# W_tok padded to 640 x 640 in a fused linear-attention and MLP kernel, with a new order for the whole program

## The chip, the cores and the metric

The kernel runs on one core of a Trainium2 chip. The core has a matrix engine (TensorE, PE in the profile; its weight loads are listed as PEld), three engines for elementwise work (VectorE or DVE, ScalarE or ACT, GpSimd or POOL) and DMA queues that are fed by SP, ACT and POOL. In this kernel matmuls write to PSUM, which the code holds as eight banks of 128 x 512 float32, and ACT and VectorE read it from there; POOL does not. The metric is the device time of one execution in microseconds (us).

## The reference

Eight batches of 576 tokens pass through linear attention with eight heads of 64 columns and then through a block that mixes tokens and channels:

```python
kv = np.einsum('bhsd,bhse->bhde', k, v)
out = np.einsum('bhsd,bhde->bhse', q, kv)
rms = np.sqrt(np.mean(out * out, axis=-1, keepdims=True) + 1e-06)
attn = out / rms * g_norm                   # heads side by side: x, 576 x 512
a1 = alpha1 * x + beta1
tok = np.einsum('ts,bsd->btd', w_tok, a1)   # w_tok is 576 x 576
u = x + lam * tok
a2 = alpha2 * u + beta2
ch = np.maximum(a2 @ w_ch1, 0.0) @ w_ch2    # 512 -> 2048 -> 512
return u + lam * ch
```

All inputs and the output are float32. The kernel multiplies in bfloat16 from the token mixing on and in float32 forms in the attention.

## The kernel before, in words

A batch has 576 = 4 x 128 + 64 tokens. Its work comes in pieces of 128 tokens (c = 0 to 3) and a tail of 64 (c = 4); the tails of two batches, an even and the odd one after it, share one piece of 128 partitions.

For every batch `kv` forms K^T V for all heads (lines 607 and 613), and ACT and VectorE bring it from PSUM into `kvc` (624, 626). `norm` multiplies q by it (697) and `norm_ops` normalises: a square on ACT (665), a sum on VectorE (668), a root on ACT (671), a reciprocal (674) and products on VectorE (676 to 683), for some pieces one on POOL (686). `tok` multiplies by W_tok transposed (780), `tok_tail` does so for the shared tail (825). `a2_dma` scales the result (870, 874, 877), and a transposing DMA brings it into `a2m`, for the tail into `a2l`. `ch1` is the first channel matmul with its relu (890 and 885, the tail 902), `ch2` the second (919, for the last piece of the last batch 930), and `finish` adds lambda times the result and stores it (947 to 955).

Batch 0 runs in two halves of four heads (j = 0, 1) so that it can begin when a part of the inputs is there: `qt_early` copies q (556 on ACT, 559 on POOL) and transposes it on TensorE (563), ACT bringing it to `qt` (576); `kv_first` makes K^T V from 64 x 64 tiles (585; copies 595 and 597); `norm_half` (723 to 759; 759 is POOL's product that writes `rm`), `tok_half` (803) and `a2_pair`, which transposes on TensorE (845), follow. Batch 1's q too goes through `qt_early`; later batches have theirs transposed by VectorE (1090).

W_tok is loaded in three DMAs from POOL (482 twice, 485) that turn it into bfloat16. `wt_group` transposes it: for each of five groups of columns four matmuls with the identity (971) and one for the last 64 rows (974). ACT and VectorE copy the result to `wt` (981, 978, 986). `wsums` (997, 999) sums it with a matmul by `pick` and writes the sums to the upper half of `wt`'s fifth tile; two DMAs (1013) then make a sixth tile, with the halves exchanged, for odd batches. Since 576 = 4 x 128 + 64, the fifth group is 64 columns wide (its 971 fill 64 of TensorE's columns) and the last 64 rows use 64 of its rows (974, 999).

w1 is loaded in four parts (1057) and w2 in four (1063), from POOL; k and v of the batches from 1 on too, each in a large and a small part (1080, 1084). SP issues batch 0's and batch 1's q (463), batch 0's k and v (463), later q (1072), the rows of constants (517, 1115), the transposes and the stores.

What decides the order is a list by hand of a planner: `ORDER`. Every operation of the program has a number in the order in which the code makes it, and `replay` puts the operations on their engines in the order of the list. `53:5:6` is operation 53 with PSUM banks 5 and 6. `206:7+325:4` is two or three groups of matmuls whose instructions are woven with each other. `~14` is fourteen filler matmuls on a constant tile (line 447; the tile `fil` is set at 446) whose result nobody reads. Each engine, and each issuer of DMAs, runs its part of the list in that order. `GATES` makes an operation wait for another one beyond what the data need, `8: 14` operation 8 for operation 14; what stands behind 8 on its issuer then waits too.

## Time and profile before

| what | us |
|---|---|
| median of 3 runs | 349.39 (349.28 to 351.33) |
| the profiled execution's own time | 349.69 |
| its span (first to last instruction) | 347.5 |
| TensorE busy | 340.9 |
| VectorE busy | 186.4 |
| GpSimd (POOL) busy | 162.4 |
| ScalarE (ACT) busy | 153.0 |
| first ch1 matmul of batch 0 starts at | 33.13 |
| first tok matmul of batch 1 starts at | 61.51 |

A row of the timeline has the start, the duration, the engine, the line, the operation, what it writes and reads, and the count of what was merged into it; behind it, in brackets, how long the engine stood idle and what ended that. A duration of several matmuls includes the end of the last, which the profile shows beyond the start of the next, so the price of a matmul is taken from one start to the next. In the chain of waits a row has start, duration, engine, tile and line.

### The profile page before, as it was taken

Reading aid. Unit: us, or ns where it says so; the run is one execution under the profiler, and the core shown is the slowest. Engines: PE = TensorE matmul, PEld = TensorE weight load, DVE = VectorE, ACT = ScalarE, POOL = GpSimd, SP = SyncE. Lnnn points to the kernel's source line nnn. Section 1 sums busy time; section 2 is a strip of 40 time slices with the busy share of each in tenths; the row PEclk is TensorE's granted clock in tenths of the full one; section 3 lists DMA queues with packets and bytes.
Section 4 is the critical chain, followed back from the end, with each engine's and each line's share of the span. In section 5 each row is a group of like instructions: output and inputs, shape, how many; then the busy total and the mean of one; then the engine's idle time right before and its main releaser. Section 6 shows DMA issues by size and latency. Waiting matters only on the chain.

```text
span 347.5 us, 5443 instructions
## 1 busy us (share of the span) xinstructions
PE 340.9 (98%) x2188; PEld 194.2 (56%) x2188; DVE 186.4 (54%) x343; ACT 153.0 (44%) x301; POOL 162.4 (47%) x154
## 2 busy tenths in 40 slices
PE   6999999999999999999999999999999999999996
PEld 4978465456645554555646545564576444444644
DVE  3188029774882687636854776359543963210044
...
GB/s 249 349 206 304 118 224 252 163 112 209 231 93 30 172 223 195 48 95 243 194 46 130 239 202 50 60 125 272 135 36 88 60 30 17 63 90 30 0 62 91
DMA packets 108496, 48.10 MB, mean 138 GB/s; under 512 B 82029, under 2 KB 101557, under 8 KB 108472
## 3 DMA queue, kind: packets, MB, share of 16 engines
...
q8 instruction: 17, 0.28, 0.4%
...
HBM read 38.82 MB, written 9.44 MB: 139 GB/s over the span
## 4 chain that ended last, share of the span: by engine, by line
PE 91%; DVE 5%; ACT 1%; DMA 1%; issue 0%; POOL 0%; DVEq 0%
PE ps L919 31%; PE ps L890 31%; PE ps L780 9%; PE ps L902 4%; PE ps L697 2%; PE ps L607 2%; PE ps L563 2%; PE ps L825 2%; PE ps L585 1%; PE ps L803 1%; PE ps L930 1%; DVE ps L676 1%; DMA a2l<-a2b 1%; DVE small L668 1%; PE ps L447 1%; PE ps L723 1%
## 5 line engine op out<-in xcount | busy, mean ns | idle before, releaser
L919 PE MATMUL ps<-w,hh 128*128 128x512 bf16 x560 | 137.2, 382 | 0.0
L890 PE MATMUL ps<-a2m,w 128*128 128x512 bf16 x512 | 120.3, 381 | 0.0
L885 ACT ACTIVATE hh<-ps 128x512 bf16<-128x512 f32 x144 | 84.3, 596 | 69.8 <-PE ps L890 61.0
L919 PEld LDWEIGHTS ps<-w,hh 128*128 128x128 bf16 x560 | 48.3, 98 | 51.0 <-issue 1.2
L890 PEld LDWEIGHTS ps<-a2m,w 128*128 128x128 bf16 x512 | 45.8, 98 | 51.1 <-ACT a2m L855 0.5
L870 POOL TENSOR_TENSOR a1f<-xm,a_bc 128x512 f32<-128x512 f32 x24 | 30.3, 1269 | 80.7 <-DVE xm L790 80.6
L947 DVE TENSOR_TENSOR tmp<-ps,lam_bc 128x512 f32<-128x512 f32 (+2 forms) x38 | 25.0, 662 | 53.8 <-PE ps L919 50.1
L697 PE MATMUL ps<-kvc,qt 128*128 128x128 f32 x140 | 46.7, 395 | 0.1
L952 POOL TENSOR_TENSOR xm<-xm,tmp 128x512 f32<-128x512 f32 x28 | 35.5, 1272 | 22.0 <-DVE tmp L947 22.0
L877 POOL TENSOR_TENSOR a2b<-a1f,b_bc 128x512 bf16<-128x512 f32 x32 | 40.2, 1272 | 7.4 <-DVE a1f L874 7.0
L607 PE MATMUL ps<-vr,kr 128*128 128x128 f32 x112 | 35.8, 394 | 0.0
L668 DVE TENSOR_REDUCE small<-sq 128x8 f32<-128x512 f32 (+1 forms) x35 | 23.6, 679 | 22.4 <-ACT sq L665 22.3
L697 PEld LDWEIGHTS ps<-kvc,qt 128*128 128x128 f32 x140 | 26.2, 195 | 9.3 <-DVE kvc L626 1.4
L665 ACT ACTIVATE sq<-ps 128x512 f32<-128x512 f32 (+1 forms) x35 | 20.7, 596 | 20.6 <-PE ps L697 20.3
L780 PE MATMUL ps<-rm,wt 128*128 128x512 bf16 x112 | 28.9, 379 | 0.4 <-DVE rtl L681 0.4
L790 DVE TENSOR_TENSOR xm<-ps,xm 128x512 f32<-128x512 f32 x24 | 16.6, 690 | 23.0 <-PE ps L780 23.0
L1093 ACT ACTIVATE qt<-qp 128x576 fp32r<-128x576 f32 x24 | 16.0, 681 | 23.6 <-DVE qp L1090 23.6
L607 PEld LDWEIGHTS ps<-vr,kr 128*128 128x128 f32 x112 | 21.3, 196 | 6.6 <-issue 1.3
L676 DVE TENSOR_TENSOR ps<-ps,small 128x512 f32<-128x512 f32 (+1 forms) x35 | 23.5, 691 | 0.5
L626 DVE TENSOR_TENSOR kvc<-ps,kvo 64x256 fp32r<-64x256 f32 x14 | 5.9, 420 | 27.5 <-ACT kvo L624 27.4
L1090 DVE STREAM_TRANSPOSE qp<-qs 128x576 f32<-128x576 f32 x24 | 17.7, 758 | 2.2 <-ACT qt L1093 1.8
L683 DVE TENSOR_TENSOR xm<-ps,g_bc 128x512 f32<-128x512 f32 x28 | 18.1, 677 | 0.1
(123 smaller groups left out, 309.9 us busy)
## 6 DMA issues: line engine op xcount, KB each, us to landing
...
vr<-in_v_dram POOLq DMA_DIRECT2D x7, 1024.0 KB, 12.1
...
```

Source lines behind the costliest of these rows:

```text
L607: P.mm("fill", 128, [lambda e, t=t, c=c, h=h, o=128 * (h % 4): e.matmul(t.ap()[:, o:o + 128], kr4[:, h, c:c + 2, :].rearrange("p c d -> p ...
L668: P.op("DVE", dve(n), lambda e: e.tensor_reduce(out=st, in_=sq[rs, s3, 0:nst, :], axis=AX.X, op=ALU.add), r=[("sq", s3)], w=[("sm", s4)])
L676: P.op("DVE", dve(n), lambda e: e.tensor_tensor(out=grp(ps()), in0=grp(ps()), in1=st[..., None].to_broadcast([rs.stop - rs.start, nst, DH] ...
L697: P.mm("fill", 128, [lambda e, p=p: e.matmul(dst(p), qt[:, p, cs], kvc[:, i, p, :], start=(p == 0), stop=(p == 3)) for p in range(4)], r=[ ...
L780: P.mm("fill", 512, [lambda e, sc=sc: e.matmul(t.ap(), wt[:, sc if sc < 4 else tw(b), 128 * c:128 * c + 128], rsrc(b, sc, al), start=(sc = ...
L870: P.op("POOL", pool(512), lambda e: e.tensor_tensor(out=a1f[:, s], in0=x, in1=a2_bc[:], op=ALU.mult), r=ks + ["a2"], w=[("a1f", s)])
L877: P.op("POOL", pool(512), lambda e: e.tensor_tensor(out=a2b[:, c], in0=a1f[:, s], in1=b2_bc[:], op=ALU.add), r=[("a1f", s), "b2"], w=[("a2 ...
L885: P.op("ACT", act(512), lambda e: e.activation(dst, t.ap(), ACT.Relu), r=[t], w=keys, pri=-1000)
L890: P.mm("main", 512, [lambda e, dj=dj: e.matmul(t.ap(), w1[:, dj, 128 * fj:128 * fj + 128], a2m[:, b % 3, dj, :], start=(dj == 0), stop=(dj ...
L919: P.mm("main", 512, [lambda e, fj=fj, t=t, c=c: e.matmul(t.ap(), (ht[:, fj, 128 * c:128 * c + 128] if c < 4 else hl[:, fj, :]), w2[:, fj, ...
L947: P.op("DVE", dve(z - a), lambda e: e.tensor_tensor(out=tmp[:, s, a:z], in0=t.ap()[:, 0:z - a], in1=lam_bc[:, a:z], op=ALU.mult), r=[t, "l ...
L952: lambda e: e.tensor_tensor(out=x, in0=x, in1=tmp[:, s, a:z], op=ALU.add),
```

## The change

The source of W_tok in SBUF becomes 640 columns wide with five row tiles of 128. The columns from 576 on, the rows from 64 on of its last tile, and the rows from 64 on of `wt`'s fifth tile are set to zero by three new memsets on VectorE (new operations 31, 32 and 33). With that the fifth group of 971 fills all 128 columns of TensorE, and 974 and the last matmul of `wsums` use all 128 rows; line 999 is gone. Buffers `qs` and `qp` shrink to what is used.

`ORDER` and `GATES` are new as a whole. From 31 on an operation's new number is the old one plus 3. Some of it in words, by new numbers: 6 to 11 and 16 to 21 are batch 0's loads of q, k and v by SP, which were 6 7 17 9 10 19 8 16 18 11 21, batch 1's 187, and 20, and are now 7 6 9 8 11 10 17 19 18 16 21 20; 22, 23 and 24 are W_tok's loads; 48 is POOL's first copy of q; 189 to 192 are batch 1's q loads (186 to 189 before). On POOL, after W_tok's loads, came w1 in four parts, then k and v, between copies of q; now come the first two products for `rm` (79, 72), the load of v (198), a copy of q, the first part of w1 (188), a product (86), three copies of q, the second part of w1 (193), the last three products (153, 160, 167), and then k (196), the small part of v, w1's third part, the small part of k, w1's fourth and w2. The fillers were 14, 5, 4, 25, 4 and 4, and are 39, 3, 4, 2 and 1. From batch 6 on the order is the old one.

In the diff the order is cut to its beginning, and lines that only give `mm` its new argument `tile`, which nothing reads when the program is built, are left out.

```diff
 ORDER = """
-14 32 3 6 4 204 7 13 17 12 1 205 9 2 0 10 30 29 ~14 19 31 28 8 5 33 16 15 34 27 18 40:1 ~5 11 46
-45 21 42:2 26 187 127 20 35 41 186 25 49:3 189 43 37 44 47:4 39 50 36 53:5:6 48 126 124:7 51:1
-~4 125 52 132:2 188 22 128:3 133 130:4 129 23 54 131 24 134:7:1 59 55 223 60 56 61 57 62 135 185
-58 190 70:4:5 140 136 141 137 215 63:2:3 142 138 71 143 139 191 84:6 108:1 85 72 90:7 91 64 109
-~25 192 73 65 193 74 66 75 86 110 87 111 92 93 ~4 89 195 67 95 77:4 113 88:5 94 100 102:6 76 68
-103 104 105 78 96:7 97 98 99 158:1 79 101 144:2:3 107 80 69 159 81 106 112 38 116:7 160 145 82
-161 224 146 115 114 165:6 117 83 162 163 147 118 151:4:5 164 148 225:1 149 152 119:7 226 166 150
-153 229:2 168:3 120 230 167 154 169 155 216 121 227:1 156 122 ~4 217:2 228 170 157 221:6 219:7
-218 171:4 222 173:5 220 172 175:1 174 176 194 178:3 177 196 179 309:0 180 197 312:2 310:6 198
-181:7 183:4 199 182 311:5 184 316 200 314 329:1 345:3 330 335:7 346 331:4 336 315 332 321 341:1
-322 337:3 342 319 338 206:7+325:4 320 207+333:5 326 208:1+339:3 334 203 123 323 340 209+343:6
-202 324 210+327:4 231 344 313 211 317 213 347:5 232 212 328 214 318 239:3 348 255:2 240 234
-263:6+352:7 241 256 257 242 247:4+351:1+355 264 243 244 258 259 265 233 260 266 271:5+356+360
-248 245 249 246 237 238 261 250 272 350:0 251 267 262 252 235 373 268 253 359 273 254 369 269
-274 349:3 275 270 276 353 277 236 278 279:2 285:4 280 281 291:6 286 282 287 297:5 292 283 288
-293 379:2+357+361 298 289 284 294 299 295 300 290 377:4+303:6 301 296 380 304 378+354+358 302
-305 306 201 307 386 381+365 388 387 308 486:5 382 390 384 389 383 484:6 385 391 392 487 488:4
-362 393 401 394 509:2 370 399 485 468:5 363 489 366 466:3 398 469 367 374 418:6+490:1+474:4 467
-375 491 419 510 395 426:5+470:0+462:7 475 420 397 421 364 471 422 371 423 400 511 463 512 425
-499:3 504:1 396 513 402:4+476:0+492:7 424 477 403 434:2+464:6+478:0 493 404 427 405 428 505 465
-500 501 479 406 514:7 407 372 429 376 430 506 409 410:6+472:0 368 408 431 494:4 411 495 507 432
-473 496 497 508 502 412 515 503 433 435 543:0 498 436 413 544 414 437 415 535:1 438 416 480:3
-439 559 521:5 481 441 560 522 440 561 550:4+536+528:3 417 562 563 565 442:2 564 566 447:6 443
-444 529 448 452:2 449 457:6 453 445 551+537+538 458 450 446 454 451 552:2+482:6 459 553 483 554
-455 530 555 557 556 523 460 558 456 524 461 575:6+516+517 525 526 576 531 574 567 518 573 577
 ...
+13 0 3 7 1 30 4 ~39 6 207 12 9 14 27 8 2 31 11 5 33 10 29 17 28 19 32 49 18 26 16 48 25 21 23
+50:2 20 22 43:1 54:3 52:4 37 56:5:6 53 15 24 ~3 51 57 55 44 127:1 45:7 58 62 59 63 60 64 130 61
+65 ~4 128 73:4:5 46 129 66:2:3 74 38 80:6 75 67 137:1:7 81 191 68 76 192 77 138 82 69 189 70 78
+83 ~2 71 135:5 79 139 131:4 143 136 140 144 133:2 141 84 34 145 85 132 87:5 111:3 112 72 88 146
+~1 99:6 35 89 100 134 113 101 105:7 93:4 142 114 102 39 94 95 106 90 116 107 96 108 40 161:1 198
+98 92 190 147:2:3 110 162 219 104 154:4:5 163 188 148 119:7 164 149 155 86 165 156 150 227 171:6
+120 166 218 157 151 121 168:1 226 158 152 193 224:7 169 172 225 232:2 159 228:3 153 233 220:7
+170 229 91:4 222:5 173 97 160 230:2 221 103 176:3 231 109 174:1 167 177 115 181:2 118 196 175
+182 117 199 178:6 183 194 223 179 314:2 180 313:5 197 315:7 195 184:1 186:6 185 200 122:3 187
+312:0 123 316 201 208 319 320 318 124 321 317 202 326 324 322 211:1+332:3 323 212+330:6
+209:5+334:4 210+328:0 335 325 213+336:4 331 236 327 203 340:2 216 214 217 234 337 215 342:7 341
+36 47 329 242:6+344:1 343 250:5+338:0 243 333 244 345 258:4+355:7 245 246 126 247
+274:1+354:2+346:3 259 41 248 251 125 42 260 206 252 261 266:6+358 347 262 263 253 339 254 348:3
+264 275 255 267 265 359 349 205 256 353:0 268 249 276 357 269 270 257 277 271 362 272 363 237
+278 279 361 273 280 350:5 281 235 282:3 288:4 283 284 294:6 351 285 289 300:5 286 295 290 306:1
+296 291 287 301 292 352:4 297 302 204 307 368 298 293 303 308 356 304 309 299 380:6+376 310 305
+382:3+360 311 383+364 238 381+372 365 239 369 481:4 240 373 465:0 374 482 485:5 366
+384+487:4+491:1 241 385 495:2 387 386 466 377 477:6 486 388 378 488 483:5 492 496 507:0 370
+497:1 484 471:7 391 398 502:4 472 489:3 389 478 397 498 490 499 399 500 503 392 504 508 400 390
+512:2 395 473:6 393 396 505 479:7 404 394 403 501 513 514 480 413:3+469:5 474 402 515 414
+405:7+475:6 470 415 506 509 416 510 406 437:1+538:5 417 418 511 407 516 421:4+539+467:0 420 401
+408 476 409 438 410 419 429:6+540 468 439 422 411 493:3 440 430 423 546:2 441 494 442 424 541
+412 431 524:7 443 432 547 433 425 434 525 436 435 553:3+548+526 426 427 444 450:6 428 554+445:1
+451 452 555:4+455:6 446 562 447 460:1 456 563 453 564 549 461 565 556+531:0 448 568 566
+557+517:6+532 462 449 457 454 560 527 569 561 463 558 533 528 567 559 458 518 464 519 529 459
 ...
 """

-GATES = {8: 14, 9: 204, 10: 1, 11: 30, 15: 204, 20: 45, 21: 7, 22: 18, 25: 41, 26: 27, 36: 7, 37: 0,
-    38: 107, 39: 9, 122: 136, 123: 197, 185: 133, 186: 204, 187: 27, 188: 126, 189: 10, 191: 3,
-    194: 122, 196: 101, 199: 120, 201: 305, 202: 149, 231: 154, 232: 198, 233: 259, 234: 348,
-    235: 267, 236: 232, 237: 348, 238: 256, 394: 387, 396: 391, 397: 287, 400: 289, 568: 459,
-    569: 526, 571: 585, 574: 562, 678: 705, 685: 705}
+GATES = {40: 1, 41: 152, 42: 183, 125: 327, 126: 246, 191: 75, 192: 15, 205: 255, 206: 244, 235:
+    262, 237: 345, 240: 268, 397: 335, 404: 290, 570: 428, 571: 432, 572: 427, 574: 550, 681:
+    708, 688: 708, 721: 741, 725: 375, 726: 627, 894: 885, 896: 523, 897: 523, 898: 545, 899:
+    887, 900: 884, 1043: 947, 1048: 1124, 1049: 954, 1050: 944}
 ...
-    def mm(self, stream, cols, fns, r=(), w=(), slow=False, after=(), margin=0.3,
-           urgent=False):
+    def mm(self, stream, cols, fns, r=(), w=(), slow=False, after=(), tile=0):
 
         o = Op("PE", "m", 0.0, 0.0, fns, self.bias, len(self.ops))
         o.form = (stream, cols, slow)
+        o.tile = tile
 ...
-        qs = sb("qs", [128, 3072], F32)
+        qs = sb("qs", [128, 2304], F32)
         qt = sb("qt", [128, 4, 640], F32R)
-        qp = sb("qp", [128, 2, 768], F32)
+        qp = sb("qp", [128, 2, 576], F32)
 ...
-        wl = hh[:, 0:2304].rearrange("p (c s) -> p c s", c=4)
-        wlt = hh[0:64, 2304:2880]
+        wl = hh[:, 0:3200].rearrange("p (c s) -> p c s", c=5)
 ...
-                wl[:, c:c + 2, :], moe_w_tok[128 * c:128 * c + 256, :].rearrange(
+                wl[:, c:c + 2, 0:576], moe_w_tok[128 * c:128 * c + 256, :].rearrange(
                     "(c p) s -> p c s", p=128)), w=[("wl", c), ("wl", c + 1)], issue=0.9)
         P.dma("POOL", "wlt", dcost(64, 150), lambda e: e.dma_start(
-            wlt, moe_w_tok[512:576, :]), w=["wlt"], issue=0.8)
+            wl[0:64, 4, 0:576], moe_w_tok[512:576, :]), w=["wlt"], issue=0.8)
 ...
+        P.op("DVE", dve(160), lambda e: e.memset(wl[:, :, 576:640].bitcast(F32), 0.0), w=["wlz"])
+        P.op("DVE", dve(288), lambda e: e.memset(wl[64:128, 4, 0:576].bitcast(F32), 0.0),
+             w=["wlz"])
+        P.op("DVE", dve(288), lambda e: e.memset(wt[64:128, 4, :].bitcast(F32), 0.0),
+             w=[("ws", 4), ("wst", 4)])
 ...
         def wt_group(sc):
             t = P.bank("any")
             n = 128 if sc < 4 else 64
-            cols = slice(128 * sc, 128 * sc + n)
+            cols = slice(128 * sc, 128 * sc + 128)
             for tc in range(4):
                 P.mm("fill", 128, [lambda e, tc=tc: e.matmul(
-                    t.ap(slice(0, n))[:, 128 * tc:128 * tc + 128], wl[:, tc, cols], idb[:],
-                    start=True, stop=True)], r=["idb", ("wl", tc)], w=[t])
+                    t.ap()[:, 128 * tc:128 * tc + 128], wl[:, tc, cols], idb[:],
+                    start=True, stop=True)], r=["idb", "wlz", ("wl", tc)], w=[t])
             P.mm("fill", 64, [lambda e: e.matmul(
-                wtt.ap(slice(0, n))[:, 64 * sc:64 * sc + 64], wlt[:, cols], idb[0:64, 0:64],
-                start=True, stop=True)], r=["idb", "wlt"], w=[wtt])
+                wtt.ap()[:, 64 * sc:64 * sc + 64], wl[:, 4, cols], idb[:, 0:64],
+                start=True, stop=True)], r=["idb", "wlt", "wlz"], w=[wtt])
 ...
-                    t.ap()[:, 0:n], pick[:, :], wt[:, sc, a:z], start=(sc == 0), stop=False)
-                    for sc in range(4)] + [lambda e, t=t, a=a, z=z, n=n: e.matmul(
-                        t.ap()[:, 0:n], pick[0:64, :], wt[0:64, 4, a:z], start=False,
-                        stop=True)],
-                    r=["pick"] + [("wtt" if a else "wt", i) for i in range(5)], w=[t])
+                    t.ap()[:, 0:n], pick[:, :], wt[:, sc, a:z], start=(sc == 0), stop=(sc == 4))
+                    for sc in range(5)],
+                    r=["pick", ("wst" if a else "ws", 4)] +
+                    [("wtt" if a else "wt", i) for i in range(5)], w=[t])
 ...
-              [("wl", c) for c in range(4)] + ["wlt"] + [("qi", 0, 0, m) for m in range(2)])
+              [("wl", c) for c in range(4)] + ["wlt", "wlz"] + [("qi", 0, 0, m) for m in range(2)])
```

16 lines of the change are left out of this document (8 added, 8 removed), and 94 rows, old and new, of the table ORDER.

## The prediction

> **What bounds the kernel now.** I read the page's sums, the table of stretches, the chain of waits in order of time, then the timeline of TensorE, ACT, VectorE and POOL where the table shows slack.
>
> ```profile
> PE 340.9 (98%) x2188; PEld 194.2 (56%) x2188; DVE 186.4 (54%) x343; ACT 153.0 (44%) x301; POOL 162.4 (47%) x154
> PE 91%; DVE 5%; ACT 1%; DMA 1%; issue 0%; POOL 0%; DVEq 0%
> ```
> ```profile
> 0.00:10.00 10.00, 7.06 (x35) 4.68 (x37) 3.22 (x12) 4.38 (x8) 5.05 (x10) 1.00 0.81 271
> 60.00:70.00 10.00, 9.60 (x49) 4.32 (x46) 7.18 (x11) 2.39 (x4) 5.71 (x5) 1.00 1.33 174
> 70.00:80.00 10.00, 9.80 (x58) 5.33 (x55) 6.90 (x11) 6.16 (x12) 3.85 (x5) 1.00 0.65 118
> 100.00:140.00 40.00, 40.00 (x211) 21.01 (x209) 25.17 (x43) 16.31 (x32) 23.49 (x21) 1.00 0.86 137
> ```
>
> The first two numbers of a stretch are its length and TensorE's busy time. From 80 us on TensorE is never without a matmul and holds the chain, so a new order there cannot gain; it can only open a gap. Gains must come from before 80 us: from gaps, from filler matmuls (L447, which keep TensorE occupied while it waits and compute nothing), and from matmuls that take longer than their kind does elsewhere.
>
> ```profile
> 0.85 0.27 DVE L502 MEMSET rtl<- 64x256 uint32 x1 [0.85 <-PEq L1187]
> 2.51 0.17 DVE L446 MEMSET fil<- 128x128 bf16 x1
> 2.73 1.67 PE L447 MATMUL ps<-fil 128*128 128x128 bf16 x14 [2.73 <-DVE fil L446]
> 4.93 0.65 POOL L559 COPY hh<-xm 128x576 f32<-128x576 f32 x1
> 11.48 1.61 POOL L482 DMA_DIRECT2D hh<-in_moe_w_tok_dram  x2 [0.33 <-DMA w<-in_k_dram]
> 18.68 1.57 PE L447 MATMUL ps<-fil 128*128 128x128 bf16 x25
> ```
> ```profile
> L485 POOL DMA_DIRECT2D hh<-in_moe_w_tok_dram x1: 556/556/556, 13.1 to 13.1; - x1
> ...
> DMA to landing us min/median/max: 6.5/6.5/6.5
> ```
> ```profile
> L463 SPq DMA_DIRECT2D xm<-in_q_dram x1: 347/347/347, 11.2 to 11.2; - x1
> ...
> DMA to landing us min/median/max: 5.3/5.3/5.3
> ```
> ```profile
> L463 SPq DMA_DIRECT2D xm<-in_q_dram x1: 394/394/394, 0.7 to 0.7; - x1
> ...
> DMA to landing us min/median/max: 3.0/3.0/3.0
> ```
>
> The start is bound by loads. SP's sixteen loads land from 0.7 + 3.0 = 3.7 us to 11.2 + 5.3 = 16.5, 0.85 apart on the mean; W_tok, issued from 11.48, has landed at 13.1 + 6.5 = 19.6. TensorE spends 1.4 us of the wait (18.68 to 20.08) on 25 fillers.
>
> **The change, part by part: first loads and W_tok.** The new order issues batch 0's twelve loads first (7 6 9 8 11 10 17 19 18 16 21 20), W_tok right after POOL's first copy, and the second batch's four q loads later. That copy waits for a q load, so W_tok's issue begins near the 5.6 us at which the copy at 4.93 ends. Twelve loads at 0.85 end at 3.7 + 11 x 0.85 = 13.1. W_tok took 19.6 - 16.5 = 3.1 more, so all is there at about 16.2 instead of 19.6. What is not shown is who goes first: W_tok is issued while SP still issues its last loads, so the last k lands between 13.1 and 16.2.
>
> The filler memset becomes VectorE's first instruction, so the 39 leading fillers can begin near 1.2 (VectorE's first starts at 0.85). At 1.67/14 = 0.12 each they end near 5.9, about when the first transposes get their inputs. They cost nothing, as the q loads cover them; without that cover they would cost 4.7.
>
> The last k starts 18 matmul pairs of L585 (1.05), nine transposes (1.1) and the twenty W_tok matmuls.
>
> ```profile
> 17.89 0.85 PE L971 MATMUL ps<-idb,hh 128*128 128x128 bf16 x6
> 21.48 0.26 PE L974 MATMUL ps<-idb,hh 64*128 64x64 bf16 x3
> 21.67 0.62 PE L971 MATMUL ps<-idb,hh 128*128 128x128 bf16 x8
> 22.10 1.05 PE L723 MATMUL ps<-kvc,qt 128*128 128x256 f32 x6
> 23.35 1.04 PE L997 MATMUL ps<-wt,pick 128*128 128x512 bf16 x4
> 30.08 1.04 PE L845 MATMUL ps<-ident,xm 128*128 128x128 f32 x8
> 33.13 1.24 PE L890 MATMUL ps<-a2m,w 128*128 128x512 bf16 x5
> ```
>
> **The padding.** Eight L971 of full width take 22.10 - 21.67 = 0.43, 0.054 each. The first six, two of them 64 columns wide, take 18.68 - 17.89 = 0.79: the two narrow ones cost (0.79 - 4 x 0.054)/2 = 0.29 each. Padded, four of these save 4 x 0.23 = 0.9. The 64-row ones (L974, L999) stand alone in the same way; with about 0.05 to 0.1 saved on each of seven, the padding is worth 1.4 us of TensorE. Three memsets are added to VectorE, which is busy for 3.2 of the first 10 us; its memsets above took 0.17 and 0.27, so 0.5 to 0.8 in all; the loads hide it, and without them it would be that much.
> The Trainium skill (TensorEngine Tiling, When to Use Tiling) speaks against it: it advises splitting the array for a dimension of 64 or less, up to 2x. By that, padding would give away about half of eleven small matmuls, an estimated 0.3 us; the 0.29 against 0.054 of this trace goes the other way, since the narrow ones here stand between full ones.
>
> Now the sum for the start. With everything there at 16.2, the last L971 ends between 18.3 (k early) and 19.5 (k late), against 22.10: 2.6 to 3.8 gained. What comes next is ACT.
>
> ```profile
> 22.33 0.60 ACT L981 ACTIVATE wt<-ps 128x512 bf16<-128x512 f32 x1 [0.31 <-PE ps L971]
> 29.39 1.29 POOL L759 TENSOR_TENSOR rm<-xm,la_bc 128x512 bf16<-128x512 f32 x1 [0.41 <-DVE xm L754]
> 18.67 0.94 POOL L1080 DMA_DIRECT2D vr<-in_v_dram  x1
> ```
>
> In the new ACT queue, eight small kvc copies, three qt copies, three wt copies and a square stand between the last L585 and the sums L997. Now wt's copies end at 22.93 and L997 starts at 23.35. Counted from a last L585 at 15 or at 17.3, the copies end near 20 or 22: 1.4 to 3.3 of the gain reach L997. From there to the first L890 both orders have the same matmuls (33.13 - 23.35 = 9.8), but POOL's last rm product may be late by then. I take **2.5** for the start, nearer the middle than either end; the ends are 0 (ACT and POOL keep everything) and 4.1 (TensorE alone decides: 18.3 plus the 11.0 that now follow 22.10, less 0.3 of narrow ones, is 29.0 against 33.13).
>
> **Batch 1 and 2, 50 to 80 us.**
>
> ```profile
> 61.51 1.04 PE L780 MATMUL ps<-rm,wt 128*128 128x512 bf16 x4 [0.41 <-DVE rtl L681]
> 66.36 0.41 PE L607 MATMUL ps<-vr,kr 128*128 128x128 f32 x1
> 66.87 0.41 PE L607 MATMUL ps<-vr,kr 128*128 128x128 f32 x1
> 67.88 0.41 PE L607 MATMUL ps<-vr,kr 128*128 128x128 f32 x1
> 70.77 0.78 PE L607 MATMUL ps<-vr,kr 128*128 128x128 f32 x5
> 71.38 0.61 PE L919 MATMUL ps<-w,hh 128*128 128x512 bf16 x2
> 77.61 0.38 PE L902 MATMUL ps<-a2l,w 128*128 128x128 bf16 x4 [0.20 <-DMA a2l<-a2b]
> ```
> ```profile
> 141.49 1.05 PE L825 MATMUL ps<-rm,wt 128*64 128x512 bf16 x8
> ...
> 142.69 1.90 PE L919 MATMUL ps<-w,hh 128*128 128x512 bf16 x8
> ```
> ```profile
> 327.18 13.81 PE ps L919 x64
> ```
>
> A 512-column matmul costs 13.81/64 = 0.216. Woven, one L607 and two L919 take 66.87 - 66.36 = 0.51, so the L607 adds 0.075; alone, five take 71.38 - 70.77 = 0.61. The token tail of batch 1 (ten L825, 64 columns wide) is woven with four L607 and takes 70.77 - 67.88 = 2.89. Batch 3's ten, alone, take 142.69 - 141.49 = 1.20. The new order has batch 1's tail alone (306 as a word of its own) and its L607 beside L919: 1.20 + 0.1 to get in + 4 x 0.075 = 1.6, so **1.3** saved. It also has no L607, L613 or L697 group alone: 28 matmuls that stood alone now are woven, at most 28 x 0.047 = 1.3; getting in and out takes some, so **1.0**. Both lie on TensorE, which is the bound there.
>
> The two gaps of 0.41 and 0.20 may go: the new order puts 32 L890 and L919 in place of 24 between the norms and L780, and the second set of q loads behind the transposes of batch 1 rather than ahead. What is late next is its gates: the copy of wt's fifth tile (126) waits for batch 1's first reciprocal, and 41, 125, 42, 206 and 205 queue behind it on SP; L780 waits for them. I let new waits of the same size as the old gaps eat those 0.6.
>
> Sum: 2.5 + 1.3 + 1.0 = 4.8. The profiled execution took 349.69 us (span 347.5 and 2.19 around it), 0.30 above the median 349.39. Forecast: 349.69 - 4.8 = **344.9**.
>
> **The rivals.**
>
> First, *TensorE decides the start*: k lands early, ACT and POOL keep up, and both gaps go. 4.1 + 1.3 + 1.0 + 0.6 = 7.0, so 342.7. For it speaks that only 10 fillers are left behind the first 39, against 33 now from 12 us on; against it the crowded ACT queue. In the trace fillers take 0.12 each at 2.73 and 1.4/25 = 0.056 at 18.68: TensorE is slow at first. The Trainium skill (TensorE: Matmul & The Clock Gate, Part 1) puts this down to a clock that opens after some 3.4 us of sustained activity; by that, an unbroken run from 1.2 would open it near 5 to 8 us, which favours this rival. My sum has no term for it, since the loads set the pace until 13.
>
> Second, *the start gives nothing back*: the loads come early, but L997 or the rm products come when they did, because ACT and POOL got more in front of them. Only 1.3 + 1.0 remain: 347.4. POOL speaks for it: v's load and four q copies stand in front of the last three products, the last of which now ends at 30.7.
>
> Third, slower: *the weights start too late*.
>
> ```profile
> L1057 POOL DMA_DIRECT2D w<-in_moe_w_ch_dram x2: 775/780/785, 16.3 to 17.1; - x2
> ...
> DMA to landing us min/median/max: 11.2/12.1/13.0
> ```
>
> Now POOL has issued all of w1, k and v by 19.6 (18.67 + 0.94), and w1 has landed at 17.1 + 13.0 = 30.1. In the new order k, half of w1 and w2 stand on POOL behind the three rm products. If these end at 30.7 as now, k lands near 36, and the stream of weights behind it near 50; TensorE wants k for its first L607, which follows 16 L890 instead of 37: at 33.13 - 2.5 + 16 x 0.216 + 1.0 for eight L845, about 35, and w2 at 45 to 60. So it decides as soon as the products end no earlier than now: from there each us of POOL is one of TensorE. To be 3.5 slower it must eat the 4.8 too, 8.3 beyond that point, with k near 44: 353 to 355, say 354. Against it: POOL gets its inputs earlier as well.
>
> **How the numbers follow.** Chances: forecast 0.35 (343.5 to 346.3), first rival 0.25, second 0.28, third 0.12. About 1% (3.5 us) is what a measurement of this kernel can tell from no change: below 345.9 lie the first rival and three quarters of the forecast, a little of the second, 0.54; above 352.9 the third, 0.13; the rest 0.33. The range 342.0 to 349.8 reaches from just past the first rival to the second with all the gaps of 50 to 80 us back; it leaves out 0.08 below and 0.12 above.
>
> **What would show it.** The first L890 near 30.6 (29.0 by the first rival, 33 by the second); the last W_tok landing near 16; narrow L971 gone, and L971 at 0.054 throughout; the tail of batch 1 in 1.2; no L607 in groups of its own; TensorE without a gap from 80 us on. I am wrong if TensorE waits for w1, w2, k or for wt's fifth tile between 25 and 60 us, or if a gap opens in the second half.

## The result, and the profile after

The changed kernel takes 347.82 us (median of 20 runs, 344.71 to 349.65), the kernel before 350.23 (median of 20 runs, 348.86 to 352.35). The ratio is 0.9924, 95% interval 0.9904 to 0.9944. So it is faster by 2.4 us between the medians (about 2.7 by the ratio), where 4.8 were forecast, and it lies 2.9 above the 344.9 of the forecast. The sign was right and the time lies in the range, but about half of the gain is missing. The profiled execution was the slowest of the 20: 349.65 us with a span of 347.5, the same span as the profile of before. That suits the question, since it shows every loss at once.

From the page of the changed kernel, TensorE's sum and the shares of the chain:

```profile
PE 337.5 (97%) x2181; PEld 194.9 (56%) x2181; DVE 187.0 (54%) x346; ACT 149.0 (43%) x301; POOL 162.0 (47%) x154
PE 81%; DMA 9%; SPq 3%; POOL 3%; DVE 2%; ACT 1%; issue 1%
```

TensorE is busy for 3.4 us less than before in a span that is as long. TensorE's share of the chain fell from 91% to 81%, and that of the DMAs rose from 1% to 9%: there is less work, and more waiting for loads. The table of stretches of the same kernel says where (behind the stretch and its length come the busy times of TensorE, its weight loads, VectorE, ScalarE and POOL; the third number from the end is the granted clock):

```profile
10.00:16.00 6.00, 3.67 (x52) 2.63 (x51) 3.89 (x12) 3.92 (x12) 2.07 (x3) 0.99 1.13 275
16.00:22.60 6.60, 5.74 (x62) 5.56 (x63) 1.45 (x8) 2.41 (x7) 6.47 (x8) 0.50 0.76 209
22.60:30.00 7.40, 6.65 (x54) 5.04 (x53) 6.54 (x15) 4.74 (x12) 1.72 (x3) 1.00 0.77 157
60.00:70.00 10.00, 10.00 (x54) 4.63 (x52) 7.67 (x12) 3.48 (x6) 6.08 (x7) 1.00 1.02 152
70.00:80.00 10.00, 10.00 (x59) 5.70 (x57) 3.28 (x6) 2.38 (x6) 4.07 (x5) 1.00 1.11 134
```

The gaps of 60 to 80 us are gone. In their place TensorE is idle for 2.3 of the 6 us from 10 to 16, the granted clock is 0.50 from 16 to 22.6, and POOL, whose products the first channel matmul needs, is busy for only 1.7 of 7.4 us from 22.6 to 30. The timeline of TensorE names the steps:

```profile
1.05 4.34 PE L445 MATMUL ps<-fil 128*128 128x128 bf16 x39 [1.05 <-DVE eps L446]
...
16.86 2.18 PE L588 MATMUL ps<-qs,w 64*64 64x64 f32 x36 [3.20 <-DMA w<-in_k_dram]
...
34.55 1.49 PE L893 MATMUL ps<-a2m,w 128*128 128x512 bf16 x6
...
60.91 1.03 PE L783 MATMUL ps<-rm,wt 128*128 128x512 bf16 x4
...
65.33 1.05 PE L828 MATMUL ps<-rm,wt 128*64 128x512 bf16 x8
...
66.53 0.82 PE L922 MATMUL ps<-w,hh 128*128 128x512 bf16 x3
...
174.40 0.30 PE L610 MATMUL ps<-vr,kr 128*128 128x128 f32 x1 [1.50 <-issue]
```

And the timeline of VectorE, SyncE and POOL behind the first half of batch 0:

```profile
20.65 0.27 DVE L505 MEMSET rtl<- 64x256 uint32 x1
20.95 1.24 SPq L520 DMA_DIRECT2D rtl<-a2m  x2
22.23 0.58 SPq L461 DMA_DIRECT2D xm<-in_q_dram  x1
28.26 0.67 POOL L562 COPY xm<-xm 128x576 f32<-128x576 f32 x1 [5.77 <-DMA xm<-in_q_dram]
...
29.70 2.53 POOL L762 TENSOR_TENSOR rm<-xm,la_bc 128x512 bf16<-128x512 f32 x2
```

And the chain of waits from the last k to that memset:

```profile
6.40 10.43 DMA w<-in_k_dram
...
20.05 0.34 ACT kvc L598 x2
...
20.42 0.23 DVE kvc L600
...
20.65 0.27 DVE rtl L505
```

Read in order, there are three losses. **First**, the last k is late: TensorE stands idle for 3.20 us until 16.86, and then the clock is halved. L588 takes 2.18 us for 36 matmuls where 36 took 1.26 at 7 us. **Second**, POOL waits 5.77 us for the fourth q load of batch 1; that load is issued only at 22.23, behind the two rows of L520, which are issued right after a memset of 0.27 us that VectorE does at 20.65. The first two losses hang together: VectorE reaches the memset only behind copies that come from the late k (L598 and L600), so a late k makes the rows and the q late too. The first L893 starts at 34.55, 1.4 later than before (33.13), where I had said 30.6. **Third**, TensorE waits 1.5 us at 174.4, where batch 5's k has just landed (159.2 + 15.1 = 174.3, shown under 12 and 13). The tail of batch 1 takes 1.2 us (65.33 to 66.53) and token mixing of batch 1 starts without a gap at 60.91, as foretold.

A second trace of the same kernel tells which of these are steady (its numbers are under the experiments): the late k and the late q come again, the gap at batch 5 doesn't.

### The profile page after: what moved, and what is told of

It is laid out like the page before. It is cut to its first block, busy times and chain, and to the rows that moved or that the text cites. A ratio compares the mean times of both kernels' runs of the same rounds, so it can differ in the third digit from the quotient of the medians.

```text
span 347.5 us, 5445 instructions
## 1 busy us (share of the span) xinstructions
PE 337.5 (97%) x2181; PEld 194.9 (56%) x2181; DVE 187.0 (54%) x346; ACT 149.0 (43%) x301; POOL 162.0 (47%) x154
## 4 chain that ended last, share of the span: by engine, by line
PE 81%; DMA 9%; SPq 3%; POOL 3%; DVE 2%; ACT 1%; issue 1%
PE ps L922 34%; PE ps L893 28%; PE ps L783 8%; PE ps L905 3%; DMA w<-in_k_dram 3%; PE ps L700 3%; DMA qs<-in_q_dram 2%; DMA kr<-in_k_dram 2%; PE ps L610 2%; DMA xm<-in_q_dram 2%; SPq L461 1%; POOL a2b L880 1%; PE ps L828 1%; SPq L1074 1%; PE ps L933 1%
## 5 line engine op out<-in xcount | busy, mean ns | idle before, releaser
L922 PE MATMUL ps<-w,hh 128*128 128x512 bf16 x560 | 137.0, 382 | 0.0
L893 PE MATMUL ps<-a2m,w 128*128 128x512 bf16 x512 | 121.9, 381 | 0.0
L888 ACT ACTIVATE hh<-ps 128x512 bf16<-128x512 f32 x144 | 81.8, 598 | 72.2 <-PE ps L893 59.0
L922 PEld LDWEIGHTS ps<-w,hh 128*128 128x128 bf16 x560 | 49.7, 98 | 53.1 <-issue 0.8
L893 PEld LDWEIGHTS ps<-a2m,w 128*128 128x128 bf16 x512 | 46.6, 98 | 51.0 <-ACT hh L888 1.2
L700 PE MATMUL ps<-kvc,qt 128*128 128x128 f32 x140 | 47.4, 408 | 0.1
L610 PE MATMUL ps<-vr,kr 128*128 128x128 f32 x112 | 36.3, 407 | 1.9 <-issue 1.5
L700 PEld LDWEIGHTS ps<-kvc,qt 128*128 128x128 f32 x140 | 27.5, 197 | 7.1 <-issue 0.4
L783 PE MATMUL ps<-rm,wt 128*128 128x512 bf16 x112 | 29.6, 381 | 0.0
L1095 ACT ACTIVATE qt<-qp 128x576 fp32r<-128x576 f32 x24 | 15.8, 680 | 29.8 <-DVE qp L1092 29.7
L793 DVE TENSOR_TENSOR xm<-ps,xm 128x512 f32<-128x512 f32 x24 | 16.4, 686 | 21.9 <-PE ps L783 21.8
L610 PEld LDWEIGHTS ps<-vr,kr 128*128 128x128 f32 x112 | 22.1, 198 | 6.5 <-issue 2.0
```

Source lines behind the costliest of these rows:

```text
L610: P.mm("fill", 128, [lambda e, t=t, c=c, h=h, o=128 * (h % 4): e.matmul(t.ap()[:, o:o + 128], kr4[:, h, c:c + 2, :].rearrange("p c d -> p ...
L700: P.mm("fill", 128, [lambda e, p=p: e.matmul(dst(p), qt[:, p, cs], kvc[:, i, p, :], start=(p == 0), stop=(p == 3)) for p in range(4)], r=[ ...
L783: P.mm("fill", 512, [lambda e, sc=sc: e.matmul(t.ap(), wt[:, sc if sc < 4 else tw(b), 128 * c:128 * c + 128], rsrc(b, sc, al), start=(sc = ...
L888: P.op("ACT", act(512), lambda e: e.activation(dst, t.ap(), ACT.Relu), r=[t], w=keys, pri=-1000)
L893: P.mm("main", 512, [lambda e, dj=dj: e.matmul(t.ap(), w1[:, dj, 128 * fj:128 * fj + 128], a2m[:, b % 3, dj, :], start=(dj == 0), stop=(dj ...
L922: P.mm("main", 512, [lambda e, fj=fj, t=t, c=c: e.matmul(t.ap(), (ht[:, fj, 128 * c:128 * c + 128] if c < 4 else hl[:, fj, :]), w2[:, fj, ...
```

## The experiments

Theory A: the start is paced by loads that come in the wrong order. The last k shares the DMA engines with W_tok, and the late k also costs the clock; batch 1's q and two rows stand behind a small memset. The rivals: POOL's and ACT's queues pace the first L893 whatever lands when; the halved clock alone is the loss; or the terms behind the start (padding, tail) were wrong. All kernels, with the ratio to the kernel before of the same group and the first L893 (in kernels built on the one before, L890 or L887) in the trace of each:

| kernel | median us (runs) | ratio, 95% interval | first L893, us | span of the trace |
|---|---|---|---|---|
| changed kernel | 347.82 (20) | 0.9924 [0.9904, 0.9944] | 34.55 | 347.5 |
| changed kernel again | 348.16 (12) | 0.9936 [0.9903, 0.9968] | 33.95 | 345.2 |
| 1 W_tok late | 346.09 (7) | 0.9923 [0.9888, 0.9958] | 29.91 | 340.7 |
| 2 fillers in the wait | 350.91 (12) | 1.0026 [1.0007, 1.0046] | 34.67 | 348.2 |
| 3 fourth q early | 347.19 (6) | 0.9920 [0.9889, 0.9951] | 33.29 | 345.7 |
| 4 = 1 + 3 | 342.48 (6) | 0.9802 [0.9767, 0.9837] | 29.46 | 340.3 |
| 4 again | 342.89 (6) | 0.9808 [0.9777, 0.9839] | 29.04 | 340.5 |
| 5 memset early | 345.84 (6) | 0.9882 [0.9857, 0.9908] | 32.78 | 343.9 |
| 6 = 1 + 5 | 343.16 (5) | 0.9799 [0.9780, 0.9818] | 29.49 | 341.1 |
| 7 = 1 + 3 + 5 | 343.00 (5) | 0.9802 [0.9778, 0.9825] | 28.54 | 339.8 |
| 8 before, padding alone | 349.97 (12) | 0.9996 [0.9971, 1.0021] | 33.08 | 347.6 |
| 9 before, tail alone | 350.88 (12) | 1.0026 [0.9996, 1.0056] | 33.47 | 349.4 |
| 10 kernel 4, tail woven | 345.08 (6) | 0.9885 [0.9847, 0.9923] | 33.63 | 345.8 |
| 11 before, early clock | 350.38 (12) | 1.0013 [0.9992, 1.0035] | 33.88 | 348.0 |
| 12 stores late | 348.34 (12) | 0.9957 [0.9935, 0.9978] | 35.29 | 347.3 |
| 13 = 4 + 12 | 343.57 (6) | 0.9815 [0.9786, 0.9844] | 29.08 | 342.7 |

**1, 3 and 4: the order of the loads.** W_tok's first issue (23) waits for the second v load (11), and a small product of POOL (37) is moved ahead of it so that it isn't held too:

```diff
-... 48 25 21 23 50:2 20 22 43:1 54:3 52:4 37 56:5:6 ...
+... 48 25 37 21 23 50:2 20 22 43:1 54:3 52:4 56:5:6 ...
-GATES = {40: 1, 41: 152, ...
+GATES = {23: 11, 40: 1, 41: 152, ...
```

> W_tok's first transfer is held on GpSimd until the second v load of batch 0 has landed (7.5 us in the changed kernel's trace), so that SyncE's twelve loads go first. Theory A (the changed kernel's start is paced by the last k load, which shares the DMA engines with W_tok, lands at 16.8 us and leaves TensorE 3.3 us idle, after which the granted clock is halved for 6.8 us): the last k lands at 13 to 14 us, W_tok at 16.5 to 18 us, no idle stretch of TensorE over 1 us from 5 to 20 us, no half clock after 6 us; first L893 at 31.5 to 33 us instead of 34.55; time 344.5 to 346 us where the changed kernel has 347.8. Rival B (the second rival of the prediction: the first hidden-layer work is paced by the queues of ACT and POOL, the start gives nothing back): last k as in A, but first L893 within 0.5 us of 34.5 and time 347.3 us or more. Rival C (the loads share alike whoever is issued first): last k still lands after 16 us, time 347.8 us.

The third moves batch 1's fourth q load (190) ahead of the rows (39, 40) on SyncE:

```diff
-... 82 69 189 70 78 ... 39 94 ... 40 161:1 198 98 92 190 147:2:3 ...
+... 82 69 189 190 70 78 ... 39 94 ... 40 161:1 198 98 92 147:2:3 ...
```

> Batch 1's fourth q load is moved on SyncE's queue ahead of the two rows (L520) that wait for VectorE's memset at 20.65 us. It then issues at about 16 us instead of 22.2 us and lands before 23 us; POOL's idle stretch of 5.8 us before its copy of that load (L562) goes to under 1 us, and the residual products, the k load and the weights behind it on POOL come 3 to 5 us earlier. Theory A (this wait is the second pace-setter of the start): TensorE's waits of 0.94 us at 28.1 and 0.53 us at 38.9 us go, time 346 to 347 us. Rival D (it is off the path: the half clock decides, and TensorE has other work): POOL's stretch goes, time within 0.4 us of 347.8.

> The first and the third experiment together: W_tok after SyncE's loads, and batch 1's fourth q ahead of the two rows. Theory A: the two gains add, 343.5 to 345.2 us, first L893 at 30.5 to 32 us. Rival B: no more than the larger of the two alone, since the queues of ACT and POOL set the first hidden-layer work: 346.5 to 347.5 us.

The load of the last k in the changed kernel, then in kernel 4 (count, duration of the issue in ns, the first and the last start; the last line is the time from issue to landing of the last v and the last k, and its largest number is k's):

```profile
L461 SPq DMA_DIRECT2D w<-in_k_dram x1: 495/495/495, 6.4 to 6.4; - x1
...
DMA to landing us min/median/max: 9.4/9.9/10.4
```

```profile
L461 SPq DMA_DIRECT2D w<-in_k_dram x1: 443/443/443, 6.8 to 6.8; - x1
...
DMA to landing us min/median/max: 7.7/7.9/8.1
```

The k that is issued at 6.4 lands 10.4 us later, at 16.8; with W_tok held it is issued 0.4 later and lands at 14.9, and W_tok itself is complete at 17.8 where it was at 17.4. So who is issued first does matter, and rival C of the first expectation falls. (The Trainium skill, DMA: Bandwidth & Descriptors, in Queues, rings and completion order, says that each DMA engine takes turns packet by packet between the queues that have work. The landings agree: with W_tok on POOL's queue from 5.2 us on, SyncE's last k landed 1.9 us later.) The waits of POOL and TensorE in kernel 4, then its timeline:

```profile
PE ps L588 <- DMA w<-in_k_dram: 1.3, 2, 0.9
```

```profile
24.26 2.52 POOL L762 TENSOR_TENSOR rm<-xm,la_bc 128x512 bf16<-128x512 f32 x2 [0.83 <-DVE xm L757]
...
29.46 1.49 PE L893 MATMUL ps<-a2m,w 128*128 128x512 bf16 x6
```

TensorE waits 1.3 us for loads of k, in two waits, 0.9 of it for the last one, instead of 3.2; POOL's last products start 5.4 us earlier than the 29.70 of the changed kernel, and the first L893 comes 5.1 earlier than in that kernel's slowest run (4.5 earlier than in its second trace). Kernel 4 is faster than both kernels: 0.980 of the time before. Its 342.48 lies below the 343.5 to 345.2 that theory A expected, and the rival's 346.5 to 347.5 is out. In kernel 1 the first L893 was earlier than expected (29.91 against 31.5 to 33), the median just later; in kernel 3 POOL's wait for q went, the first L893 came at 33.29, and the time fell between the two theories.

What theory A had wrong is that the gains add: by the ratios each edit alone gives next to nothing (0.9923 and 0.9920 against 0.9924 and 0.9936 of the changed kernel; by the medians 346.09 and 347.19 against 347.8 to 348.2), and together they give 5 us. What POOL's last products wait for in kernel 3, then the memset and POOL's copy of the fourth q in kernel 1:

```profile
POOL rm L762 <- DVE xm L757: 3.5, 1, 3.5
```

```profile
16.76 0.27 DVE L505 MEMSET rtl<- 64x256 uint32 x1
```

```profile
23.63 0.67 POOL L562 COPY xm<-xm 128x576 f32<-128x576 f32 x1 [1.73 <-DMA xm<-in_q_dram]
```

With the q early and the k late (kernel 3), POOL has its q but waits 3.5 us for VectorE's products of batch 0's second half, which stand behind the late k: one wait takes the place of the other. With the k early and the q behind the rows (kernel 1), this trace shows nothing of the kind: the memset comes 3.9 us sooner by itself, POOL waits 1.7 us instead of 5.8, and the first L893 starts at 29.91. But the trace is of the fastest of its seven runs, 342.8 us; four more take 345.5 to 347.1, two 348.5 and 348.8. Where those lose their time no trace shows; 5 to 7 bear on it.

**2 and 11: the clock by itself.** Fillers during the wait for the last k (138 is the product that needs it):

```diff
-... 192 77 138 82 ...
+... 192 77 ~58 138 82 ...
```

> 58 filler matmuls (56 ns each at full clock, 3.2 us) stand on TensorE's queue between the third and the fourth group of the first key-value products, so that TensorE runs while it waits for the last k; nothing of the loads is changed. Theory A says that of the loss behind the wait, the half clock is one part: the last k still lands at about 16.8 us, the granted clock stays full from 5.6 us on, the products of L588, L566 and L977 take their full-clock times (L977 56 ns instead of 107); time 345.5 to 346.5 us, the spread of the runs smaller. If the half clock is not what costs (rival: POOL's wait for batch 1's q at 22.5 to 28.3 us hides it), the time stays at 347.5 to 348.2 us although the clock is full.

And the kernel before with an early start of the fillers:

```diff
-14 32 3 6 4 204 7 13 17 12 1 205 9 2 0 10 30 29 ~14 19 ...
+14 0 32 3 6 4 204 7 13 17 12 1 205 9 2 10 30 29 ~39 19 ...
```

> The kernel before with the filler memset as VectorE's first instruction and 39 fillers in place of the first 14, so that TensorE runs from 1.05 us on; nothing of the loads or of the other queues is changed. Theory A (the start is paced by the loads, W_tok lands at 19.6 us as before): the granted clock may open near 6 us instead of 12.6, but the first L890 stays within 0.5 us of 33.1 and the time within 0.7 us of the kernel before. Rival (the early clock by itself is worth time): first L890 1 to 2 us earlier, time 348 to 349 us where the kernel before has 349.9.

From the stretches, the waits and the timeline of the kernel with fillers in the wait:

```profile
16.00:22.60 6.60, 6.54 (x106) 6.05 (x103) 2.77 (x11) 3.77 (x11) 6.22 (x8) 1.00 0.85 242
```

```profile
POOL xm L562 <- DMA xm<-in_q_dram: 6.2, 1, 6.2
```

```profile
34.67 1.06 PE L893 MATMUL ps<-a2m,w 128*128 128x512 bf16 x4
...
88.06 0.33 PE L700 MATMUL ps<-kvc,qt 128*128 128x128 f32 x1 [0.86 <-ACT qt L1095]
...
197.24 0.60 PE L893 MATMUL ps<-a2m,w 128*128 128x512 bf16 x2 [1.58 <-DMA a2m<-a2b]
```

The clock stayed full and the first L893 came no earlier, since POOL waits for its q as long as before. (The 58 fillers ran until 17.47, where the last k had landed at 16.6, so they also held its products back by some 0.9 us.) So the halved clock was real but covered by the other wait, as the rival said. The ratio is 1% above that of the changed kernel, which neither theory expected. Its trace has gaps of 0.86 and 1.58 us, at 88 and 197 us, that the changed kernel's traces lack; whether these are what all its runs have is open.

For the kernel before with early fillers, TensorE's timeline and one stretch:

```profile
9.46 1.26 PE L585 MATMUL ps<-qs,w 64*64 64x64 f32 x36 [1.51 <-DMA w<-in_k_dram]
...
33.88 1.24 PE L890 MATMUL ps<-a2m,w 128*128 128x512 bf16 x5
```

```profile
10.00:16.00 6.00, 5.55 (x101) 5.04 (x98) 0.22 (x2) 2.45 (x6) 5.46 (x8) 0.72 1.08 356
```

L585 now runs at full clock at 9.46, but it had to wait for its k; the clock fell once more between 10 and 16, and the first L890 starts at 33.88, 0.75 later than in the trace of before, where theory A had allowed 0.5. An early clock that isn't kept is worth nothing here (1.0013), as theory A said of the time; one that stays full in the old order was not tried.

**5, 6 and 7: the memset.** What held the rows and the q behind them is VectorE's memset of `rtl` (35). It is moved ahead of the first halves:

```diff
-... 28 19 32 49 18 ... ~1 99:6 35 89 ...
+... 28 19 32 35 49 18 ... ~1 99:6 89 ...
```

> The changed kernel with one thing moved: VectorE's memset of rtl (L505, 0.27 us) from its place behind the normalisation of batch 0's first half (20.65 us) to the first loads' wait (about 4 us). If the memset holds the rows and the q load behind them (theory A'): the two rows issue near 15 us and land before 20 us, the fourth q lands near 20.5 us instead of 28.3, POOL's wait of 5.8 us goes, first L893 at 32.5 to 33.5 us instead of 34.55; the last k is as late as before (16.8 to 18 us) with its idle stretch and half clock; time 1 to 2 us below the changed kernel (ratio to the kernel before 0.987 to 0.991). Rival (the rows are held by something else on SyncE): q as late as before, ratio 0.992 to 0.994.

> W_tok after SyncE's loads, and the memset of rtl early; the fourth q keeps its place behind the rows. Theory A': the same as with the q ahead of the rows, first L893 at 28.8 to 30 us and ratio 0.976 to 0.982, with a spread of the runs of 4 us or less; the wide spread of the first experiment (342.8 to 348.8 us) came from rows and q that sometimes land late. Rival: the spread stays, ratio 0.988 to 0.994 as in the first experiment.

> All three edits: W_tok after SyncE's loads, the fourth q ahead of the rows, the memset early. Theory A': rows land by 19 us in every run, no run over 344 us on a fast chip, median 341 to 342.7 us, ratio 0.974 to 0.980; first L893 at 28.8 to 29.6 us. Rival: the memset's place does not matter once q is ahead of the rows, ratio 0.980 to 0.982 as without it.

The waits and TensorE's timeline of kernel 5:

```profile
PE ps L588 <- DMA w<-in_k_dram: 3.3, 2, 2.7
```

```profile
32.78 1.50 PE L893 MATMUL ps<-a2m,w 128*128 128x512 bf16 x6
```

Theory A' holds for kernels 5 and 6. In kernel 5 the rows are issued at 15.8 and the fourth q at 17.1, and POOL no longer waits for it: moving 0.27 us of VectorE is worth 0.4 to 0.5% with the late k still there. With W_tok late as well (kernel 6) it gives 0.9799, five runs from 342.2 to 343.2, while W_tok late alone was 0.9923, five of its seven runs from 342.8 to 347.1. For kernel 7 the rival holds: the three together are no better than any pair with W_tok late, 0.9802. Five runs are few to tell a spread by (kernel 4, its memset late, has twelve from 341.3 to 345.1). One way in which late rows can cost time is seen in kernel 10, below, that trace's rows and the wait for them, then POOL's load of v beside them:

```profile
L520 SPq DMA_DIRECT2D rtl<-a2m x2: 631/1096/1562, 17.7 to 18.4; - x2
...
  PE ps L806: 2.7, 1
...
DMA to landing us min/median/max: 2.9/5.3/7.7
```

```profile
17.69 0.95 POOL L1082 DMA_DIRECT2D vr<-in_v_dram  x1
```

The first row, issued with the load of v, lands after 2.9 us. The second is issued 0.66 us after the beginning of that load; its issue takes 1.56 us instead of 0.63 and it lands after 7.7, and TensorE waits 2.7 us for it. The traces of kernels 1, 4 and 13 agree: rows issued ahead of that load by 0.5 to 0.7 us, or within 0.1 us of its beginning, took 2.0 to 3.0 us, and the one that came 0.77 after it 5.2. But in kernels 5 to 7 rows issued 1.7 to 2.8 us ahead of the load took 3.1 to 5.8, so the load of v isn't all that a row can meet. Those rows had landed by 21.8 us, and TensorE waited for none of them. That late rows slowed kernel 1's other runs is likely, but no trace of one of them shows it.

**8, 9 and 10: padding and tail.** Padding alone is the changed code with the list of before, its numbers from 31 on raised by 3, and the three memsets put behind 5 on VectorE:

```diff
-14 32 3 6 4 204 7 ... 28 8 5 33 16 15 34 ...
+14 35 3 6 4 207 7 ... 28 8 5 31 33 32 36 16 15 37 ...
```

> Only the padding of W_tok with its three memsets, in the order, banks and gates of the kernel before. My reading (a narrow matmul between full ones costs 0.29 against 0.054 us): the transposes L974 and L977 and the sums L1000 together take 1.2 to 1.6 us less on TensorE, but they wait for W_tok, which lands when it did; time 0.3 to 1.4 us below the kernel before, 348.0 to 349.1 us where that has 349.4. By the rule that padding of a dimension of 64 gives time away: 0.3 us more than before, 349.7 us.

```profile
18.49 0.57 PE L968 MATMUL ps<-idb,hh 128*128 128x128 bf16 x6
...
33.08 1.24 PE L887 MATMUL ps<-a2m,w 128*128 128x512 bf16 x5
```

The six transposes take 0.41 from their start to the next instruction (18.90) where they took 0.79, so each of the two narrow ones gave 0.19, near the 0.23 of my price. But the first L887 starts at 33.08 against 33.13, and the time is the same (0.9996): nothing that can be seen reaches the end. In this order TensorE runs 25 fillers for W_tok between the transposes, and the sums behind them start at 23.40, as before at 23.35. The two starts aren't a clean pair, since in this trace k's last products began 0.7 us later than before (14.48 against 13.75). Of the expected 0.3 to 1.4 us the medians show none, nor the loss of 0.3 by the other rule; the interval (1.0 us faster to 0.7 slower) leaves room for a part of either.

The tail of batch 1 taken apart in the kernel before, and woven again in kernel 4 (two banks change so that the unit fits at its place, and 477 goes two places later):

```diff
-... 295 300 290 377:4+303:6 301 296 ...
+... 295 300 290 303:6 377:4 301 296 ...
```

> The kernel before, with one unit of the order taken apart: the token tail of batch 1 (ten L825 of 64 columns) stands alone ahead of the four L607 that were woven with it. My term of the sum was 1.3 us with those L607 beside L919; here they stand alone in one group at 0.11 us each, so the pair costs 1.20 + 0.1 + 0.45 = 1.75 us in place of 2.89: 1.1 us faster, 348.3 us where the kernel before has 349.4; the ten L825 take 1.2 us in the trace. If the price of changing width is not what the weaving cost, the time stays within 0.3 us of the kernel before.

```diff
-... 295 290 306:1 296 ... 309 299 380:6+376 310 305 382:3+360 ... 377 477:6 486 388 ...
+... 295 290 380:3+306:1 296 ... 309 299 376 310 305 382:6+360 ... 377 486 388 477:6 ...
```

> The yardstick with the token tail of batch 1 woven again with four L610, as in the kernel before, and the L922 that these were woven with alone. Prediction's term: 1.3 us; theory A (nothing waits behind the tail in the new order, so the term is real): 1.0 to 1.5 us slower than the yardstick, the tail's stretch about 2.9 us in the trace instead of 1.2. Rival (as in the kernel before with the tail taken apart, a wait for the transposed pieces of batch 1 behind it takes up the difference): within 0.4 us of the yardstick.

In the kernel before with the tail apart, and in kernel 4 with the tail woven:

```profile
68.29 1.05 PE L825 MATMUL ps<-rm,wt 128*64 128x512 bf16 x8
...
74.60 0.60 PE L890 MATMUL ps<-a2m,w 128*128 128x512 bf16 x2 [0.76 <-DMA a2m<-a2b]
```

```profile
63.27 0.41 PE L610 MATMUL ps<-vr,kr 128*128 128x128 f32 x1
...
66.16 2.12 PE L922 MATMUL ps<-w,hh 128*128 128x512 bf16 x9
```

In the old order, the tail's 1.2 us is there (68.29 to 69.49), but TensorE now reaches the first channel matmul of batch 1 too early and waits 0.76 for its transposed piece, and 0.76 once more at 102, for VectorE. No gain: 1.0026. In the new order, weaving the tail again makes it 2.89 us (63.27 to 66.16) and the time 2.2 us longer than kernel 4 of the same group (345.08 against 342.89). That is more than the 1.0 to 1.5 expected; the late row of 2.7 us in its trace, the one shown above, says that the difference isn't the tail's alone. So the term was real in the new order; the stretches of the traces give it 1.3 (2.89 less 1.20, less the 0.4 that the prediction gives the four L610 beside L922), the medians up to 2.2.

**12 and 13: batch 5's k.** Two stores (544, 537) that go out beside batch 5's k and v are moved behind the last q load (726), on the changed kernel and on kernel 4:

```diff
-544 742 ... 802:3 723 537 751 ... 726 731 732 ...
+742 ... 802:3 723 751 ... 726 544 537 731 732 ...
```

> The changed kernel with two of the stores of batch 1 (L963 and one L959), which are issued at 159.1 and 162.3 us beside batch 5's loads of k and v, moved on SyncE's queue behind the last of batch 5's q loads. Theory A: batch 5's k (issued at 159.2) then lands in 9 to 12 us instead of 15.1, before TensorE wants it at 172.5; the gap of 1.66 us before batch 5's first L610 is gone in the trace, nothing opens in its place, and the time is 1 to 1.7 us below the changed kernel of this group. Rival: the loads of q and v alone keep the DMA engines busy, k lands as late, or the moved stores make a buffer late and a gap of the same size opens behind 175 us: same time.

> The yardstick with the two stores of batch 1 moved behind batch 5's last q load as well. Theory A, in the form that batch 5's k is late because of these stores in some executions: the slow end of the yardstick's runs goes, median 0.3 to 1 us below the yardstick. After the trace of the stores moved alone (k landed 13.8 us after its issue instead of 15.1) I hold the rival likelier: the loads of q and v themselves keep the DMA engines busy, time within 0.5 us of the yardstick.

The load of batch 5's k in the changed kernel, then in kernel 12 (the last number is k's time to landing), and the first L610 of that batch in kernels 12 and 13:

```profile
L1082 POOL DMA_DIRECT2D kr<-in_k_dram x1: 888/888/888, 159.2 to 159.2; - x1
...
DMA to landing us min/median/max: 11.4/13.2/15.1
```

```profile
L1082 POOL DMA_DIRECT2D kr<-in_k_dram x1: 886/886/886, 160.3 to 160.3; - x1
...
DMA to landing us min/median/max: 9.7/11.7/13.8
```

```profile
174.13 0.30 PE L610 MATMUL ps<-vr,kr 128*128 128x128 f32 x1 [0.16 <-issue]
```

```profile
169.58 0.30 PE L610 MATMUL ps<-vr,kr 128*128 128x128 f32 x1 [1.50 <-issue]
```

In kernel 12's trace k lands 1.3 us sooner after its issue and the gap is down to 0.16, but the changed kernel's second trace has no gap either, without the edit (12.7 us to landing). In kernel 13 k takes 15.1 us again and the gap is as long as ever. The times don't move (348.34 against 348.16, 343.57 against 342.89). That the two stores cause this gap falls. Why k takes 15 us there in some executions stays open.

The yardsticks of the second and the third group:

> The changed kernel itself once more, as the yardstick of this group and for a second trace of it. Theory A (the late last k, TensorE's idle stretch before it and the halved clock behind it, POOL's wait for batch 1's q, and batch 5's k each cost time, and the runs differ by which of them strike): 347 to 348.5 us; a trace of a run near 345 to 347 us has the last k near 16 to 17 us again, but a shorter stretch of half clock or none, or no gap at batch 5's first L610. If its trace shows the same three stretches as the first one and yet a time 2 us or more lower, theory A does not explain the spread.

> W_tok after SyncE's loads and batch 1's fourth q ahead of the two rows, once more: the yardstick of this group, and a test of whether the gain stands in other executions. Theory A: 341 to 344 us, ratio to the kernel before within 0.977 to 0.984, last k at 13 to 15 us, granted clock full from 6 us on. If the first result was luck in the draw of the loads' landings: 344.5 us or more.

Both came as expected. The changed kernel's second trace was of a run of 347.33 us: the last k at 17.2 us, a wait of 2.9 for it, half a clock for a shorter time (0.74 on the mean over 16 to 22.6), the q late again, no gap at batch 5, the first L893 at 33.95. Over its 32 timed runs the mean granted clock was below 0.997 in all but four, and those four lay between 344.7 and 347.8.

## Why the prediction failed at the start and held in the middle, point by point

**The start, forecast -2.5, is the step that failed.** It came out at +0.8 to +1.4 (33.95 and 34.55 against 33.13). The sentence "what is not shown is who goes first, so the last k lands between 13.1 and 16.2" took 16.2 as the worst end, as if all twelve loads and W_tok only had to share a fixed sum of time. In six traces with W_tok early (the changed kernel's two, and kernels 2, 3, 5 and 12) the last k landed at 16.6 to 18.0. W_tok's last part landed at 17.4, not near 16, so the sum of time was too short by 1.2 too; but the larger error is that the last k came near the end of it. With W_tok held (kernels 1, 4, 6, 7 and 10) that k landed at 13.5 to 14.9. More was missing behind it. I had no term for TensorE standing idle for 3 us, and none for the clock that falls after it. And I followed POOL's and ACT's queues but not SyncE's: I listed q as four loads "later", without asking what stands in front of the fourth, which was two rows that wait for a memset that the new order had moved from VectorE's first place to 20.65 us. And in its new place the memset comes behind the late k, so one late load made the other.

**The gain of the start was there once the loads go as I had assumed.** Kernel 4 has its first L893 at 29.46, kernel 7 at 28.54; I had 30.6, and 29.0 for the first rival. So 2.5 was even modest: 3.7 to 4.6 us were there, the latter more than the 4.1 of my upper end, and the change as made left them lying.

**The second rival** ("the start gives nothing back", 347.4) came nearest. Its time was met within 0.5 us, its place (the rm products on POOL) too; what held POOL was not its own queue but SyncE's. That its time fits is luck in part: it has 0 for the start and 2.3 for the middle, and the start lost 0.8 to 1.4 while the middle gained 3.1.

**The middle, forecast -2.3, came out at -3.1.** From the first channel matmul to the end of the span: 347.5 - 33.13 = 314.4 before, 345.2 - 33.95 = 311.3 in the second trace of the changed kernel, and 347.5 - 34.55 - 1.7 for batch 5's gap = 311.3 in the first (1.7 because the 1.50 of the profile begins only where the last matmul's end is shown; at 0.216 a matmul the four from 171.88 on are through at 172.74). The two old gaps went and nothing took their place there, so the 0.6 that I gave to new waits was too careful; 2.3 + 0.6 = 2.9. The tail (-1.3) is confirmed by taking it back; the 28 lone matmuls (-1.0) were not tried alone.

**A gap in the second half**, which I had named as what would make me wrong, opened in some executions at batch 5. It costs 1.5 us there; the k lands after 15.1 us in all three traces that have it (the changed kernel's first, kernels 3 and 13), and why it does isn't known.

**The padding** did to TensorE what I said, and in the old order nothing that shows in the time. I had not put it into the sum as a term of its own, and that was right.

**The clock.** The first rival's mechanism is half true. The 39 fillers take 0.11 each and at 7 us the products run at full clock (36 L588 in 1.26). From the some 3.4 us of the Trainium skill (TensorE: Matmul & The Clock Gate, Part 1) I had worked out, as an estimate, 5 to 8 us, and the trace agrees. But the early clock was worth nothing in kernel 11, and here it was lost again in the wait for k. (Behind 12 us the order of before has 4 + 25 + 4 + 4 = 37 fillers, not the 33 that I counted; nothing hangs on it.) The third rival, late weights, stayed small: TensorE waited 0.37 us for batch 1's k until 39.66, one of the waits that I had named as a sign of being wrong.

The sum: -3.1 for the middle and +0.8 for the start give -2.3, which is the difference of the two spans by construction; the medians differ by 2.4.
